# A gated mix of two attentions on one core: tiles of the second half of the values prepared before the weights are loaded, zero rows sent later and from more partitions, two SBUF pools in another order

## The chip, the cores and the metric

The kernel runs on one core of a Trainium2 chip. The metric is the device time of one execution in microseconds. The kernel before took 1667.22 us, the median of three executions (1666.85 to 1672.58). The profile is of one execution with a span of 1664.9 us.

## The reference

Two attention layers read the same input `x` (2048 tokens of 576 values, bf16) and are mixed by a gate.

```python
g = sigmoid((x * gate_w).sum(-1))
a = _A_ref(x, A_mem0, A_Wq, A_Wk, A_Wv, A_Wo, A_seg_len)
b = _B_ref(x, B_wqkv, B_wo)
return g * a + (1 - g) * b
```

- Layer A goes through the tokens in 64 segments of 32, one after the other. To each segment the 8 memory rows that the segment before produced are prepended. Those 40 rows are projected to queries, keys and values (32 heads of 128), attended under a causal mask that always admits the memory rows, and projected back by `Wo`. The first 8 output rows are the next segment's memory. So the segments form a chain.
- Layer B is ordinary full attention over all 2048 tokens with 32 heads of 18 values each. Queries, keys and values are `x @ wqkv`, without a mask, and the output is multiplied by `wo`.

## The kernel before, in words

**Two layers, interleaved.** The order of the instructions on each engine is the order in which the program writes them. Layer A's chain leaves PE idle, so layer B's attention is cut into 512 steps (`b_steps`, a generator) and the steps are placed between layer A's. A step is a block of scores (4 matmuls `sb`, L238), an exponential on ACT (`etb`, L257) and, one step later, 4 matmuls with the values (`ob`, L222). `b_advance` takes one step; `between(cost)` takes one whenever enough cost has been added up.

**The prologue** is everything before the loop over segments, up to about 225 us. This is where the change lies. In order:

1. Loads of `x` by rows of 128 tokens (`xn`, five buffers in pool `pw`) and of B's weights `wb` (L370, L371).
2. Zeros: `zt`, a `stg` tile (three buffers in pool `pw`), is cleared in 4 partitions (L377). Queries and keys of B are kept in DRAM (`qtd`, `ktd`) in groups of four heads, each head in 32 rows of which 18 are used. The other 14 rows of each head of group 0 are zeroed from `zt` by two transfers from POOL's queue, each of 4 heads by 14 rows of 4 KB (L383). POOL then issues five small transfers of `gw` and clears four tiles `vt` (pool `pp`, L392, L393); an entry of 1 in each head's 19th place makes the values' matmul give the softmax sums.
3. A loop over t = 0 to 3, 512 tokens each. `transpose_x` transposes `x` into `xT` and POOL stores it to `xtd` and copies the last 8 tokens of each segment to `xL`. `project_qk` computes blocks 0, 4 and 5 (`FIRST`) of queries and keys with 5 matmuls into a bank `pq` (L422) and casts them to a `stg` tile. `project_vb(0, kb)` computes the first half of the values, 16 heads, with 5 matmuls into `pvb` (L449), casts them into one of the tiles `vts`, and SP stores the tile to `vgd` (L457). Three PSUM banks are used in turn by all of these. Casts go to DVE or ACT by a counter (`copy_out`, L289 and L291).
4. `load_first` puts on SP the loads of the first keys, values and queries of B.
5. Layer A's weights `wv`, `wq`, `wk`: 18 pieces, 14.2 MB, issued by POOL (L106, L108). `in_turn` lets each piece wait until the piece two before it has landed; the first ones wait for the last load of point 4.
6. The gate: 80 small matmuls (L490).
7. `store_qk` of `FIRST` for groups 1 to 7: 15 stores from `stg` on SP.
8. Five more tiles for the values, in the buffers of `xn`, are cleared by POOL (L518, L519). With the four `vt` there are nine. Then `project_vb(1, kb)` for 16 kb computes the second half of the values, starting with the five new tiles.
9. Blocks 1, 6, 2, 7, 3, 8 of queries and keys, 4 times 5 matmuls each, with a step of B between some of them. After each block SP stores it to all groups.
10. The prologue's pools `pw` and `pp` are given back. `wo` (pool `aw2`), `fix` and `seg2` take memory that overlaps theirs, so a first write into them waits for the last reader of the tile that was there.
11. `last_tokens(0)`: layer A's queries, keys and values of the last 8 tokens of 16 segments (L313, L326), cast into `tm` tiles of pool `seg2`.

Every engine and every queue takes its instructions in order, so an instruction that waits holds back all behind it on the same engine. POOL's order in points 5 and 8 is: 18 weight pieces with their waits, then the memsets.

Of the kernel before, what the change touches and what calls it, by code (L numbers as in the profile page):

```python
# [9 lines left out]
BF16 = mybir.dt.bfloat16  # L10
# [6 lines left out]
def kernel(  # L17
# [15 lines left out]
    nc = tc.nc  # L33
    P = nc.NUM_PARTITIONS

    B_, S, Dm = A_x.shape
# [7 lines left out]
    DhB = Dm // HB  # L44
# [37 lines left out]
    qtd = dpool.tile([GB, P, S], BF16, name="qtd")  # L82
    ktd = dpool.tile([GB, P, S], BF16, name="ktd")
# [44 lines left out]
    def bank(k, shape, dtype, name):  # L128

        if k is None:  # L130
            k = turns[0] % 3
            turns[0] += 1
        return ps_a.tile(shape, dtype, name=name, tag=f"b{k}")
# [132 lines left out]
    def load_first():  # L266
        next(bgen)
# [17 lines left out]
    def copy_out(out, in_, share):  # L285

        evac[0] += 1
        if share and evac[0] % share == 0:
            nc.scalar.copy(out=out, in_=in_)  # L289
        else:  # L290
            nc.vector.tensor_copy(out=out, in_=in_)  # L291
# [3 lines left out]
    def load_xlb(q):  # L295
        if q < n_seg // SG:
            xlbs[q] = fil.tile([P, NF + 2, P], BF16, name="xlb", bufs=1)
            nc.sync.dma_start(out=xlbs[q][:, :, :].rearrange("p c t -> p (c t)"), in_=xld[q])
# [53 lines left out]
        ready.append(dma)  # L352

    pctx = ExitStack()
    pp = pctx.enter_context(tc.tile_pool(name="pp", bufs=1, side="right"))
    pw = pctx.enter_context(tc.tile_pool(name="pw", bufs=2, side="right"))
    xT = pp.tile([P, NF + 2, S], BF16, name="xT")
    wb = pp.tile([P, NF + 1, 3 * Dm], BF16, name="wb")
    xL = pp.tile([P, NF + 2, n_seg * LO], BF16, name="xL")
# [3 lines left out]
    def load_x(n, eng):  # L363
        xns[n] = pw.tile([P, Dm], BF16, name="xn", bufs=5)
        eng.dma_start(out=xns[n][:], in_=x_td[n * P:(n + 1) * P, :])
# [8 lines left out]
    nc.vector.memset(xT[0:TL, NF + 1, :], 0.0)  # L374

    zt = pw.tile([P, S], BF16, name="stg", bufs=3)
    nc.vector.memset(zt[0:4, :], 0.0)  # L377

    def pads(t, g):
        return t[g].rearrange("(j r) s -> j r s", r=32)[:, DhB:32, :]  # L380

    for t in (qtd, ktd):
        nc.gpsimd.dma_start(out=pads(t, 0), in_=zt[0:4, :].unsqueeze(1).to_broadcast([4, 32 - DhB, S]))  # L383
    nc.vector.memset(gw[:], 0.0)
    for c in range(NF + 1):
        n = min(P, Dm - c * P)
# [1 line left out]
    HV = HB // 2  # L388
    vts = []
    for i in range(4):  # L390
        vt = pp.tile([P, HV, 32], BF16, name=f"vt{i}")[:, :, :]
# [5 lines left out]
    def transpose_x(n):  # L397
        xn = xns.pop(n)
        ptx = bank(None, [P, NF + 2, P], BF16, "ptx")
        for c in range(NF):  # L400
            nc.tensor.transpose(out=ptx[:, c, :], in_=xn[:, c * P:(c + 1) * P], identity=ident[:, :])
        nc.tensor.transpose(out=ptx[0:TL, NF, :], in_=xn[:, NF * P:Dm], identity=ident[:, :])
        nc.tensor.transpose(out=ptx[:, NF + 1, :], in_=xn[:, T0:Dm], identity=ident[:, :])
        t = slice(n * P, (n + 1) * P)
        nc.vector.tensor_copy(out=xT[:, 0:NF, t], in_=ptx[:, 0:NF, :])
        nc.scalar.copy(out=xT[0:TL, NF, t], in_=ptx[0:TL, NF, :])
        nc.scalar.copy(out=xT[TL:P, NF + 1, t], in_=ptx[TL:P, NF + 1, :])
        nc.gpsimd.dma_start(out=xtd[n].rearrange("p (c t) -> p c t", t=P), in_=xT[:, :, t])
        nc.gpsimd.tensor_copy(
            out=xL[:, :, n * sn * LO:(n + 1) * sn * LO].rearrange("p c (s t) -> p c s t", t=LO),  # L410
            in_=xT[:, :, t].rearrange("p c (s t) -> p c s t", t=seg)[:, :, :, seg - LO:seg],
        )
# [4 lines left out]
    def project_qk(blk, t, share):  # L417
        if t == 0:
            stgs[blk] = pw.tile([P, S], BF16, name="stg", bufs=3)
        pq = bank(None, [P, QC], FP32, "pq")  # L420
        for c in range(NF + 1):
            nc.tensor.matmul(  # L422
                pq[:, :],
                lhsT=wb[:, c, blk * P:(blk + 1) * P],
                rhs=xT[:, c, t * QC:(t + 1) * QC],
                start=(c == 0),
                stop=(c == NF),
            )
        copy_out(stgs[blk][:, t * QC:(t + 1) * QC], pq[:, :], share)

    def store_qk(blk, groups):
        f = blk * P
        while f < (blk + 1) * P:
            which, h, e = f // Dm, f % Dm // DhB, f % DhB
            n = min(DhB - e, (blk + 1) * P - f)
            r = 32 * (h % 4) + e
            if h // 4 in groups:
                nc.sync.dma_start(
                    out=(qtd, ktd)[which][h // 4, r:r + n, :], in_=stgs[blk][f - blk * P:f - blk * P + n, :]
                )  # L440
            f += n


    def project_vb(hf, kb, share):
        vt = vts[(kb + 4 * hf) % len(vts)]
        pv = bank(None, [P, QC], FP32, "pvb")
        c0 = 2 * Dm + hf * HV * DhB
        for c in range(NF + 1):
            nc.tensor.matmul(  # L449
                pv[:, 0:HV * DhB],  # L450
                lhsT=xT[:, c, kb * P:(kb + 1) * P],
                rhs=wb[:, c, c0:c0 + HV * DhB],
                start=(c == 0),
                stop=(c == NF),
            )
        copy_out(vt[:, :, 0:DhB], pv[:, 0:HV * DhB].rearrange("p (h e) -> p h e", e=DhB), share)
        nc.sync.dma_start(  # L457
            out=vgd[kb, :, hf * HV * 32:(hf + 1) * HV * 32], in_=vt.rearrange("p h e -> p (h e)")
        )
# [4 lines left out]
    for t in range(NQC):  # L464
        for n in range(4 * t, 4 * t + 4):
            if n + 4 < NT:
                load_x(n + 4, nc.sync)
            transpose_x(n)
        nc.gpsimd.dma_start(
            out=xld[t].rearrange("p (c t) -> p c t", t=P), in_=xL[:, :, t * P:(t + 1) * P]  # L470
        )
        if t == 0:
            load_xlb(0)
        for blk in FIRST:
            project_qk(blk, t, 2)
        if t == NQC - 1:
            for blk in FIRST:
                store_qk(blk, (0,))
        for kb in range(4 * t, 4 * t + 4):
            project_vb(0, kb, 2)  # L480

    load_first()
    ready.extend([first_loads[-1]] * 2)
# [28 lines left out]

    for blk in FIRST:
        store_qk(blk, range(1, GB))

    for i in range(5):
        vt = pw.tile([P, Dm], BF16, name="xn", bufs=5)[:, 0:HV * 32].rearrange("p (h e) -> p h e", e=32)
        nc.gpsimd.memset(vt, 0.0)  # L518
        nc.gpsimd.memset(vt[:, :, DhB:DhB + 1], 1.0)  # L519
        vts.append(vt)  # L520
    for kb in range(NKB):
        project_vb(1, kb, 3)
    for blk in (1, 6, 2, 7, 3, 8):
# [9 lines left out]
    for q in range(4):  # L533
        in_turn(
            nc.gpsimd.dma_start(
                out=wo[:, 8 * q:8 * q + 8, :], in_=A_Wo[8 * q:8 * q + 8].rearrange("h e d -> e h d")
# [34 lines left out]
    for jj in range(2):  # L571
# [3 lines left out]
            out=cap[o:o + 64, M:L],  # L575
            in_=cap[o:o + 64, M:L],
# [7 lines left out]
            out=cap[o:o + 64, 0:M],  # L584
            in_=cap[o:o + 64, 0:M],
# [460 lines left out]
    for s in range(n_seg):  # L1046
# [6 lines left out]
        for jj in range(2):  # L1053
            nc.sync.dma_start(
                out=v_sb[64 * jj + CT:64 * jj + L, :],
                in_=vld[s * LO:(s + 1) * LO, jj * (HD // 2):(jj + 1) * (HD // 2)],
# [75 lines left out]
```

The softmax here doesn't subtract the row's maximum and nothing guards it: scores larger than these inputs give would overflow.

## Time and profile before

| | |
|---|---|
| median of three executions | 1667.22 us |
| span of the profile | 1664.9 us |
| PE busy | 1476.0 us, 89% |
| ACT busy | 1140.1 us, 68% |
| DVE busy | 960.2 us, 58% |
| POOL busy | 335.8 us, 20% |
| 225 to 1600 us: PE busy, DMA share | 1295.76 of 1375 us, 0.20 |
| 60 to 120 us: PE busy, DMA share | 1.12 of 60 us, 0.80 |

How to read the profile: the page cuts the span into 40 slices of 41.6 us and gives the busy share of each engine in tenths. A table of stretches gives for chosen windows the busy time of each engine with the number of instructions, then the granted clock of PE, the mean share of the 16 DMA engines in use and GB/s. A line of waits reads: who waited (engine, tile, line), for whom, the total in us, how often, the longest. A line in order of time gives start, duration, engine, line, operation, out<-in, and in brackets the idle time before it and what ended it.

### The profile page before, as it was taken

How to read it: one execution, taken by the hardware profiler on the slowest of the kernel's cores; microseconds unless marked ns; L12 is line 12 of the kernel's file. 1: busy time of each engine (PE TensorE's matmuls, PEld its weight loads, DVE VectorE, ACT ScalarE, POOL GpSimd, SP SyncE). 2: the span in 40 equal slices, each digit the busy share in tenths (PEclk: the TensorE clock that was granted, in tenths of full speed). 3: DMA queues.
4: the chain of work that ended last, by engine and by line, in shares of the span. 5: the costliest groups of instructions: out<-in, count | busy, mean ns of one | idle time of the engine just before them, and what ended most of it. 6: DMA issues, size and time to landing. Idle time of an engine off the chain costs nothing.

```text
span 1664.9 us, 57761 instructions
## 1 busy us (share of the span) xinstructions
PE 1476.0 (89%) x25082; PEld 781.3 (47%) x25082; DVE 960.2 (58%) x2355; ACT 1140.1 (68%) x981; POOL 335.8 (20%) x725
## 2 busy tenths in 40 slices
PE   5409789999999999999999999999999989998987
PEld 3204354455555444555545444555554444444445
DVE  2104356666656666666656666666666666565656
ACT  2105567677767777777767777777777788778784
POOL 4320121121313121121213121212121212111031
PEclk9759899999999999999999999999999999999999
DMA  6773532211212212221112122211212121211125
GB/s 177 245 261 99 198 95 63 66 47 44 51 45 49 52 36 59 44 52 39 43 38 65 35 47 51 46 46 35 59 40 51 32 46 30 49 30 33 28 58 162
DMA packets 210089, 114.39 MB, mean 69 GB/s; under 512 B 159715, under 2 KB 197475, under 8 KB 208243
## 3 DMA queue, kind: packets, MB, share of 16 engines
q1 hardware_dynamic: 188971, 58.40, 15.8%
q0 software_dynamic: 19920, 50.02, 9.4%
q8 instruction: 196, 3.21, 0.8%
q10 hardware_dynamic: 944, 2.29, 0.4%
q14 instruction: 58, 0.48, 0.1%
HBM read 60.94 MB, written 36.10 MB: 58 GB/s over the span
## 4 chain that ended last, share of the span: by engine, by line
PE 69%; ACT 11%; DVE 11%; DMA 5%; issue 2%; POOL 1%; SPq 1%; ACTq 0%; DVEq 0%; POOLq 0%
PE pvv L755 26%; ACT etb L257 8%; PE sb L238 8%; PE ob L222 7%; PE pt L782 5%; PE pv L326 4%; PE psh L800 3%; PE acc L643 3%; PE pso L838 2%; PE pq L422 2%; PE pv L313 2%; DVE hl L657 2%; DVE ot L850 2%; DVE hl L654 2%; ACT rq L830 2%
## 5 line engine op out<-in xcount | busy, mean ns | idle before, releaser
L257 ACT ACTIVATE etb<-sb 128x2048 bf16<-128x2048 f32 x512 | 959.6, 1874 | 343.7 <-PE sb L238 343.7
L767 DVE CAST tm<-pvv 128x512 bf16<-128x512 f32 x384 | 264.4, 689 | 173.7 <-PE pvv L755 172.6
L755 PEld LDWEIGHTS <-ht 128*32 128x32 bf16 x7680 | 185.6, 96 | 183.6 <-DVE ht L891 14.1
L238 PE MATMUL sb<-qch,kch 32*128 32x512 bf16 x2048 | 203.7, 386 | 37.7 <-ACT etb L257 35.7
L222 PE MATMUL ob<-etb,vch 128*32 128x512 bf16 x2048 | 206.2, 392 | 0.8 <-DVE tq L159 0.8
L850 DVE CAST ot<-pso 128x320 bf16<-128x320 f32 x256 | 120.7, 488 | 104.8 <-PE pso L838 100.5
L643 PE MATMUL acc<-wo,ot 128*32 128x384 bf16 (+1 forms) x4096 | 160.3, 291 | 5.5 <-DVE ot L850 3.3
L755 PE MATMUL pvv<-wq_m,ht 128*32 128x512 bf16 x2048 | 134.6, 383 | 13.0 <-DVE ht L891 8.5
L755 PE MATMUL pvv<-wv_m,ht 128*32 128x512 bf16 x2048 | 134.5, 383 | 0.0
L755 PE MATMUL pvv<-wk_m,ht 128*32 128x512 bf16 x2048 | 133.5, 381 | 0.0
L643 PEld LDWEIGHTS <-ot 128*32 128x32 bf16 x4096 | 105.4, 98 | 46.7 <-DVE ot L850 12.9
L700 POOL DMA_DIRECT2D a_dram<-rl x186 | 92.6, 506 | 163.9 <-DVE rl L695 143.3
L238 PEld LDWEIGHTS <-kch 32*128 32x128 bf16 x2048 | 61.1, 91 | 126.7 <-issue 106.5
L857 POOL COPY otl<-ot 128x256 bf16<-128x256 bf16 x64 | 25.9, 405 | 445.1 <-DVE ot L850 445.1
L222 PEld LDWEIGHTS <-vch 128*32 128x32 bf16 x2048 | 52.9, 93 | 118.0 <-issue 116.2
L782 PE MATMUL pt<-ident,tm 128*128 128x128 bf16 x1024 | 96.8, 221 | 0.8 <-DVE tm L767 0.8
L838 PE MATMUL pso<-et,v_sb 64*128 64x40 bf16 x2048 | 81.4, 178 | 14.3 <-DVE hll L657 5.3
L790 DVE COPY kt<-pt 128x512 bf16<-128x512 bf16 x128 | 54.0, 422 | 69.4 <-PE pt L782 69.1
L838 PEld LDWEIGHTS <-v_sb 64*128 64x128 bf16 x2048 | 62.9, 93 | 62.0 <-issue 49.8
L654 DVE CAST hl<-acc 128x384 bf16<-128x384 f32 (+1 forms) x128 | 57.9, 452 | 57.7 <-PE acc L643 57.5
L782 PEld LDWEIGHTS <-tm 128*128 128x128 bf16 x1024 | 57.8, 98 | 67.0 <-issue 49.4
L826 ACT ACTIVATE lt<-pss 128x320 f32<-128x320 f32 x128 | 56.0, 438 | 43.4 <-PE pss L822 32.8
(141 smaller groups left out, 1841.2 us busy)
## 6 DMA issues: line engine op xcount, KB each, us to landing
v_sb<-tm SPq DMA_DIRECT2D x512, 32.0 KB
wo<-in_A_Wo_dram POOLq DMA_DIRECT2D x4, 1152.0 KB, 8.6
wv_m<-in_A_Wv_dram POOLq DMA_DIRECT2D x4, 1024.0 KB, 7.6
wq_m<-in_A_Wq_dram POOLq DMA_DIRECT2D x4, 1024.0 KB, 5.4
wk_m<-in_A_Wk_dram POOLq DMA_DIRECT2D x4, 1024.0 KB, 5.8
xl<-qld SPq DMA_DIRECT2D x64, 64.0 KB
xl<-kld SPq DMA_DIRECT2D x64, 64.0 KB
v_sb<-vld SPq DMA_DIRECT2D x128, 32.0 KB
```

What stands on the lines that cost most here:

```text
L222: nc.tensor.matmul(ob[32 * j:32 * j + 32, :], lhsT=vc[:, o + 32 * j:o + 32 * j + 32], rhs=et4[:, j, :], start=(kb == 0), stop=(kb == NKB - 1),
L238: nc.tensor.matmul(sb[:, j, :], lhsT=kc[32 * j:32 * j + 32, o:o + P], rhs=qch[gq][32 * j:32 * j + 32, :], start=True, stop=True, tile_posi ...
L257: nc.scalar.activation(out=before[:, :, :], in_=sb[:, :, :], func=ACT.Exp, scale=scale_b)
L326: nc.tensor.matmul(pv[:, o:o + P], lhsT=lw, rhs=xlb[:, cc, :], start=(c == 0), stop=(c == NF))
L643: nc.tensor.matmul(acc[32 * j:32 * j + 32, 0:d1 - d0], lhsT=o[:, h, 0:CT], rhs=wo[:, h, d0:d1], start=(b == 0 and i == 0), stop=(b == 1 an ...
L654: nc.vector.tensor_copy(out=hl[:, 0, d0:d1], in_=acc[:, 0:d1 - d0])
L700: eng.dma_start(out=rows4[m, seg - LO:seg, i * n:(i + 1) * n], in_=rl[32 * i + m * LO:32 * i + (m + 1) * LO, :],)
L755: nc.tensor.matmul(pv[32 * j:32 * j + 32, :], lhsT=ht[:, cc, :], rhs=rw, start=(c == 0), stop=(c == NF), tile_position=(0, 32 * j),)
L767: nc.vector.tensor_copy(out=sbt[x][:, :], in_=ps[x][:, :])
L782: nc.tensor.transpose(out=pt[:, which, :, :, :].rearrange("p j (u i) t -> p j u i t", i=4)[:, :, :, i, :], in_=sbt[x][:, i * Dh:(i + 1) * Dh],
L838: nc.tensor.matmul(pso[:, i * L:(i + 1) * L], lhsT=v_sb[64 * jj:64 * jj + 64, b * 1024 + i * Dh:b * 1024 + (i + 1) * Dh], rhs=et[64 * jj:6 ...
L850: nc.vector.tensor_copy(out=ot[:, j * HG:(j + 1) * HG, :].rearrange("p h t -> p (h t)"), in_=ps["o", b, jj][:, 0:W8],)
```

## The change

Four edits, all in the prologue; what is computed stays the same.

- The five further tiles for the values are cleared before `load_first` and before the weights' pieces in the program's order, so on POOL the memsets stand ahead of the pieces. They are meant to be ready when the second half of the values is projected.
- The zero rows of group 0 are sent after the first four tiles of `x` have been stored (inside the loop, at t = 0), in eight transfers of 14 rows.
- Each of these reads 14 partitions of the zero tile instead of 4 partitions that are read 14 times; the tile is cleared in 14 partitions.
- Pool `pw` is opened before pool `pp`, which exchanges their places in SBUF, and with that which later tiles lie on whose old bytes.

```diff
     pctx = ExitStack()
+    pw = pctx.enter_context(tc.tile_pool(name="pw", bufs=2, side="right"))
     pp = pctx.enter_context(tc.tile_pool(name="pp", bufs=1, side="right"))
-    pw = pctx.enter_context(tc.tile_pool(name="pw", bufs=2, side="right"))
...
     zt = pw.tile([P, S], BF16, name="stg", bufs=3)
-    nc.vector.memset(zt[0:4, :], 0.0)
+    nc.vector.memset(zt[0:32 - DhB, :], 0.0)
...
-    for t in (qtd, ktd):
-        nc.gpsimd.dma_start(out=pads(t, 0), in_=zt[0:4, :].unsqueeze(1).to_broadcast([4, 32 - DhB, S]))
...
         if t == 0:
             load_xlb(0)
+            for r in range(8):
+                nc.gpsimd.dma_start(out=pads((qtd, ktd)[r // 4], 0)[r % 4], in_=zt[0:32 - DhB, :])
...
+    for i in range(5):
+        vt = pw.tile([P, Dm], BF16, name="xn", bufs=5)[:, 0:HV * 32].rearrange("p (h e) -> p h e", e=32)
+        nc.gpsimd.memset(vt, 0.0)
+        nc.gpsimd.memset(vt[:, :, DhB:DhB + 1], 1.0)
+        vts.append(vt)
 
     load_first()
     ready.extend([first_loads[-1]] * 2)
...
     for blk in FIRST:
         store_qk(blk, range(1, GB))
-
-    for i in range(5):
-        vt = pw.tile([P, Dm], BF16, name="xn", bufs=5)[:, 0:HV * 32].rearrange("p (h e) -> p h e", e=32)
-        nc.gpsimd.memset(vt, 0.0)
-        nc.gpsimd.memset(vt[:, :, DhB:DhB + 1], 1.0)
-        vts.append(vt)
     for kb in range(NKB):
         project_vb(1, kb, 3)
```

## The prediction

> **What bounds the kernel now.** I read the page's slices first, then the busy table of single stretches, the waits, the chain of waits and the queues.
>
> ```profile
> PE   5409789999999999999999999999999989998987
> ...
> 60.00:120.00 60.00, 1.12 (x10) 0.76 (x8) 0.17 (x1) 0.00 (x0) 9.81 (x19) 0.54 0.80 276
> 120.00:132.00 12.00, 11.14 (x67) 7.81 (x67) 4.65 (x11) 2.00 (x5) 2.90 (x10) 0.72 0.50 166
> 132.00:172.00 40.00, 37.43 (x233) 14.01 (x231) 16.99 (x25) 26.28 (x14) 0.36 (x1) 1.00 0.26 79
> 172.00:182.50 10.50, 3.72 (x27) 1.40 (x27) 0.00 (x0) 3.75 (x2) 2.36 (x3) 0.79 0.81 270
> ```
>
> From slice 5 on PE is nine tenths busy: the 64 segments are bound by PE, and the change doesn't touch them. The holes are in the prologue. The columns of the stretches are PE, PEld, DVE, ACT and POOL busy, then PE clock, DMA share, GB/s. From 60 to 120 us every engine but POOL stands still while 276 GB/s come in (the A weights); at 172 there is a second hole. A time saved before 225 us is saved at the end, as the segments run the same work from wherever they start.
>
> The waits name the causes (engine and line, waited for: total, times, longest):
>
> ```profile
> DVE xn L291 <- POOL xn L518: 61.2, 3, 60.2
> PE pvb L449 <- DVE xn L291: 59.7, 1, 59.7
> PE pq L422 <- DMA wb<-in_B_wqkv_dram: 14.6, 4, 9.5
> POOL xtd L408 <- DMA qtd<-stg: 11.5, 1, 11.5
> DVE tm L291 <- DMA ktd<-stg: 10.7, 1, 10.7
> ```
>
> The first two are the big hole: the second half's projections wait for a memset, not for weights. POOL's order of time shows why:
>
> ```profile
> 119.26 0.52 POOL L108 DMA_DIRECT2D wk_t<-in_A_Wk_dram  x1 [2.66 <-DMA wk_m<-in_A_Wk_dram]
> 119.77 0.54 POOL L518 MEMSET xn<- 128x512 bf16 x1
> 120.37 0.17 POOL L519 MEMSET xn<- 128x16 bf16 x1
> ```
>
> The memset stands behind the 18 weight issues, each of which waits for the piece two before it. PE then runs from 120.86. The third wait is the loading of wb; the last is the hole at 172: `tm` (pool seg2) lies on bytes of the old `stg` tiles, so its cast waits for their last store.
>
> From 18 to 20 us (queue: packets, MB, share of 16 engines) only the zero rows on q0 keep the queues busy:
>
> ```profile
> q0 software_dynamic: 12, 0.05, 41.7%
> q1 hardware_dynamic: 13, 0.01, 2.1%
> q10 hardware_dynamic: 5, 0.01, 1.7%
> ```
>
> That is 0.417 x 16 x 2 / 12 = 1.1 us a packet on 6.7 engines; q10 carries the end of wb. From 3 to 7 us q10 took 0.676 x 64 / 404 = 0.11 us a packet.
>
> [...] So SP's small stores will share with 8 KB weight rows; the trace has that at 72 to 76 us. [...]
>
> **The change part by part**, in times of the kernel before.
>
> (a) Zero rows. Gone: two transfers before wb. By 12 us 3.1 MB had moved, nearly all of x and wb, so wb should be in at about 13 us, not 24. New: eight 14-row transfers behind the first four xtd stores, and the cast of block 5 at t = 0 needs the zero tile's buffer (three `stg` buffers: zero, 0, 4, then 5 on the zero's). DVE waits there, and behind it stand the casts that free PE's banks. POOL: gw issues end at 7.3 instead of 8.8 (0.80 + 0.64 less), four memset pairs 2.7 us to 10.0, four store and copy pairs at 1.0 to 14.5, xld to 15.5, eight issues at 0.55 to 0.8 to 19.9 or 21.9, landing 2.6 (as xtd) to 3.5 us (as an 18-row store): 22.5 to 25.4. The cast ended at 29.35; now 23.2 to 26.1. Gain 3.3 to 6.2, taken 5. Ends: 0 if the rows move at the old 40 GB/s, 8 if the Pool part is quicker. The larger memset costs nothing: 0.91 us for 4 partitions, as for 64 (L373).
>
> (b) Memsets ahead of the weights. 5 x 0.7 = 3.5 us of POOL after the last xld (56.5), done by 60. The weights don't start later: POOL stood 12.1 us before L106, waiting for the first key and value loads. PE can run the second half from 59. Its nine tiles (five xn, four vt) take kb 0 to 8; kb 9 needs kb 0's store landed, and that store stands on SP behind 15 stores of FIRST, issued until 71.5. In the trace those go on landing until about 80 under the weights' first pieces (q1 48 packets at 74 to 76, 52 at 76 to 78). So kb 9 at 80, and one tile for each store landed up to kb 15. [...] Unhindered 0.56 us (issue pace at L457)[...]. Estimate 1.5: part of the time q0 has gaps. 80.5 + 6 x 1.5 = 89.5. The half ended at 131.9: gain 42. Ends: 79 (stores land 2.5 us after issue) and 97.5 (2.9 each), so 53 and 34.
>
> (c) Blocks 1, 6, 2, 7, 3, 8: 40 us as before (PE 37.4 of 40), now under weight traffic. Block 7 needs block 1's stores landed 13 us after it ended; under `wo` a block's stores took 10.6 us (171.8 to 182.4). Loss 2, ends 0 and 6.
>
> (d) Pool order. `tm` now lies where pp's tiles were, read long ago; instead `wo` waits for `stg`'s last store, which only moves a load needed 60 us later. 10.7 us go, less the three banks that PE filled meanwhile (3 x 1.1 us, part paid): gain 8, ends 6 and 10.7.
>
> (e) Warmer PE at 182 (clock 0.79 for 10 us): 1.5. The rest is order and names: nothing.
>
> Sum: 5 + 42 - 2 + 8 + 1.5 = 54.5; 1667.2 - 54.5 = 1612.7, say 1613. All low ends: 0 + 34 - 6 + 6 + 0 = 34, 1633. All high: 8 + 53 + 10.7 + 1.5 = 73, 1594.
>
> Do the weights then become the bound? They landed at about 122. SP's 4.2 MB beside them (16 x 128 KB and four blocks' stores), at 375 GB/s, add at most 11: 133. The path reaches `last_tokens` at 90 + 42 = 132; wv and wq are in by then, wk is used some 22 us later. Slack 20 us, so no.
>
> **The rivals.**
> 1. SP's stores starve behind the weights until these end (128 to 133): block 7 waits for block 1's stores until 130, three blocks of 6.6 follow, 150 instead of 171.8. 22 + 5 + 8 = 35: 1632. For: q1 fell to 16 packets in 72 to 74. Against: few were left to send; q0 has gaps. Chance 0.18.
> 2. The weights are slowed by over 25 us and `last_tokens` waits for wk: 1640. For: DMA share is 0.80 already. Against: the slack above. 0.05.
> 3. Slower. The zero rows' new wait on DVE, with 40 GB/s, delays t = 0 by some 5 us, and the freed window stays closed by another wait on POOL or SP: 1672. For: DVE and SP serve in order, and six more POOL issues stand ahead. Against: no queue entry ahead of the memsets depends on the weights. 0.03.
> 4. No change because what fills the window is taken back by the segments: they would have to be bound by a transfer, but have a DMA share of 0.20 and PE at 94%. 0.02.
>
> **How the numbers follow.** Forecast 0.72 at 1613; the range reaches to rival 1 and near to the high ends: 1597 to 1632. Faster by over 0.5%: 0.72 + 0.18 + 0.05 = 0.95; same 0.02; slower 0.03.
>
> **What would show it.** PE idle at 60 to 120 broken up: projections of the second half up to kb 8 by about 60, a wait of DVE or ACT for a vgd store (not POOL) of 10 to 20 us, pq blocks from about 85. DVE's wait for `qtd<-stg` in t = 0, wb in at 13 us. No wait of `tm` for `ktd<-stg`. The weights' last issue a few us later than 119. I am wrong if blocks 7, 3, 8 show long waits for stores (rival 1), if L313 or L326 wait for a weight load (rival 2), or if the segments' part is no longer 1375 us for the same work.

## The result, and the profile after

The changed kernel takes 1618.32 us (median, 1615.62 to 1619.57), beside 1669.9 us of the kernel before on the same chip: ratio 0.9687, 95% interval 0.9658 to 0.9716. That is 51.6 us less, between 47 and 57 by the interval. Forecast were 1613 us and 54.5 less, with a range of 1597 to 1632. The profiled span fell from 1664.9 to 1613.9 us.

First the page's PE slices of the changed kernel, then its table of stretches (PE, PEld, DVE, ACT and POOL busy, PE clock, DMA share, GB/s):

```profile
PE   6598899999999999999999999999999989998997
```

```profile
57.00:66.00 9.00, 5.88 (x48) 4.56 (x47) 2.36 (x6) 1.03 (x3) 0.00 (x0) 1.00 0.75 213
66.00:80.00 14.00, 1.16 (x6) 0.70 (x6) 0.92 (x2) 0.40 (x1) 2.17 (x4) 0.50 0.91 298
80.00:100.00 20.00, 18.42 (x110) 7.90 (x108) 8.10 (x13) 9.79 (x6) 2.69 (x5) 0.92 0.92 317
100.00:120.00 20.00, 18.95 (x122) 7.08 (x119) 8.30 (x12) 13.60 (x8) 2.68 (x5) 1.00 0.79 262
120.00:140.00 20.00, 15.08 (x88) 5.55 (x87) 7.45 (x13) 10.81 (x6) 3.96 (x6) 0.95 0.85 298
```

The 60 us in which only POOL worked have shrunk to a hole of 16 us in PE's work, from 63 to 79 us. From 80 on PE computes while the weights come in. From the seventh slice on, the PE slices are what they were but for one digit.

The waits of the changed kernel up to 190 us that the argument needs:

```profile
ACT xn L289 <- DMA vgd<-xn: 17.8, 1, 17.8
DVE xn L291 <- DMA vgd<-xn: 16.9, 2, 16.7
PE pvb L447 <- DVE xn L291: 16.0, 1, 16.0
DVE stg L291 <- DMA ktd<-stg: 8.0, 1, 8.0
DVE tm L291 <- DMA qld<-tm: 7.2, 4, 2.5
DVE tm L291 <- DMA vld<-tm: 4.3, 1, 4.3
PE pq L420 <- DMA wb<-in_B_wqkv_dram: 3.9, 4, 2.0
```

The wait for POOL's memset is gone, and so is `tm`'s for `ktd<-stg`; `ktd<-stg` appears instead at the cast of block 5, which waits for the zero rows (the forecast had named `qtd<-stg`; the rows of `ktd` go last). In place of the memset the tenth value tile (kb 9) waits for a store, 17 us instead of 60. And `tm` waits for the stores of `last_tokens` itself. In the order of time the new hole looks like this, on DVE and then on POOL:

```profile
61.15 0.46 DVE L291 CAST vt<-pvb 128x288 bf16<-128x288 f32 x1 [0.84 <-PE pvb L447]
78.33 0.46 DVE L291 CAST xn<-pvb 128x288 bf16<-128x288 f32 x1 [16.71 <-DMA vgd<-xn]
```

```profile
55.56 0.53 POOL L484 MEMSET xn<- 128x512 bf16 x1
56.14 0.17 POOL L485 MEMSET xn<- 128x16 bf16 x1
66.37 1.11 POOL L106 DMA_DIRECT2D wv_m<-in_A_Wv_dram  x2 [10.05 <-DMA vch<-vgd]
```

The memsets end at 56; POOL still stands 10 us before the first weights, so they cost nothing.

To see where the time came from I read when the same five instructions start in the two traces:

| point (us) | before | after | earlier by |
|---|---|---|---|
| first transpose of the loop's second round | 30.91 | 26.41 | 4.5 |
| last cast of the values' second half | 131.93 | 86.13 | 45.8 |
| last cast of blocks 1 to 8 | 171.10 | 123.42 | 47.7 |
| end of `last_tokens` (memset of `cap`, L568) | 221.95 | 170.28 | 51.7 |
| first cast of segment 0 (L767) | 228.69 | 176.17 | 52.5 |
| end | 1664.9 | 1613.9 | 51.0 |

From the first cast of segment 0 to the end it is 1436.2 us before and 1437.7 after. In all the kernels below it is 1436 to 1442, so differences are read at the points of the prologue, and a difference of 2 or 3 us between medians says little. The points themselves come from one trace each, and they scatter too: the kernel with `wo` held back (below) is the same program up to the end of the blocks, and its trace has the last cast of the values' second half at 88.3 us and the last cast of the blocks at 127.25, that is 2.2 and 3.8 us later than the changed kernel's. A difference of up to 4 us at one point doesn't count by itself.

### The profile page after: what moved, and what is told of

Same layout as the page of the kernel before. It is cut to its first block, busy times and chain, and to the rows that moved or that the text cites. A ratio compares the mean times of both kernels' runs of the same rounds, so it can differ in the third digit from the quotient of the medians.

```text
span 1613.9 us, 57766 instructions
## 1 busy us (share of the span) xinstructions
PE 1476.7 (91%) x25082; PEld 782.0 (48%) x25082; DVE 960.0 (59%) x2355; ACT 1139.8 (71%) x981; POOL 338.4 (21%) x731
## 3 DMA queue, kind: packets, MB, share of 16 engines
q10 hardware_dynamic: 944, 2.29, 0.4%
## 4 chain that ended last, share of the span: by engine, by line
PE 69%; ACT 11%; DVE 11%; DMA 4%; issue 2%; SPq 1%; POOL 1%; DVEq 0%; ACTq 0%; POOLq 0%
PE pvv L755 27%; ACT etb L257 9%; PE sb L238 8%; PE ob L222 7%; PE pt L782 5%; PE pv L326 4%; PE psh L800 3%; PE acc L643 3%; PE pso L838 3%; PE pv L313 2%; DVE hl L657 2%; PE pq L420 2%; DVE hl L654 2%; DVE ot L850 2%; ACT rq L830 2%
## 5 line engine op out<-in xcount | busy, mean ns | idle before, releaser
L767 DVE CAST tm<-pvv 128x512 bf16<-128x512 f32 x384 | 264.4, 689 | 175.1 <-PE pvv L755 174.2
```

Of the source, the lines that this page charges most:

```text
L767: nc.vector.tensor_copy(out=sbt[x][:, :], in_=ps[x][:, :])
```

## The experiments

**One part at a time.** Each of the first three is the kernel before with one of the edits that the diff shows; the fourth is the changed kernel without one.

Memsets alone:

```diff
+    for i in range(5):
+        ...
+        nc.gpsimd.memset(vt, 0.0)
+        nc.gpsimd.memset(vt[:, :, DhB:DhB + 1], 1.0)
+        vts.append(vt)
     load_first()
...
     for blk in FIRST:
         store_qk(blk, range(1, GB))
-    for i in range(5):
-        ...
-        nc.gpsimd.memset(vt, 0.0)
-        nc.gpsimd.memset(vt[:, :, DhB:DhB + 1], 1.0)
-        vts.append(vt)
```

> The kernel before with only the memsets of the five tiles moved ahead of the weights. Theory (the gains add up by stage): the second half of the values gains 40 us and the blocks after it 2, the zero rows and the wait of tm for ktd<-stg stay, so 40 to 44 us less than before, about 1626. Rival (the pool order is needed to harvest it): under the weights the stores of stg land so late that tm's wait grows from 10.7 to over 20 us, and the gain is 30 us or less, about 1638.

1628.58 us, ratio 0.9751 (0.973 to 0.9772): 41 us less. As in the theory; the rival's long wait didn't come:

```profile
DVE xn L291 <- DMA vgd<-xn: 19.7, 3, 16.7
DVE tm L291 <- DMA ktd<-stg: 9.4, 1, 9.4
```

So this edit is four fifths of the gain, the wait for the store belongs to it, and `tm`'s old wait stays at 9.4 us. From the last cast of the blocks to the end of `last_tokens` it takes 50.9 us, as in the kernel before.

Zero rows alone:

```diff
-    nc.vector.memset(zt[0:4, :], 0.0)
+    nc.vector.memset(zt[0:32 - DhB, :], 0.0)
...
-    for t in (qtd, ktd):
-        nc.gpsimd.dma_start(out=pads(t, 0), in_=zt[0:4, :].unsqueeze(1).to_broadcast([4, 32 - DhB, S]))
...
             load_xlb(0)
+            for r in range(8):
+                nc.gpsimd.dma_start(out=pads((qtd, ktd)[r // 4], 0)[r % 4], in_=zt[0:32 - DhB, :])
```

> The kernel before with only the zero rows' edit. Theory: wb lands by 13 us, the loop starts its second round about 4 us earlier, and so does all that follows, the weights too: 3 to 4 us less than before. Rival (the wait for the weights hides it): no change, 0 to 1 us.

1665.18 us, ratio 0.9978 (0.9968 to 0.9989): 4 us less. The second round starts at 27.07 us (30.91 before) and segment 0's first cast at 225.97 (228.69). So the wait for the weights doesn't hide the gain.

Pools alone:

```diff
-    pp = pctx.enter_context(tc.tile_pool(name="pp", bufs=1, side="right"))
     pw = pctx.enter_context(tc.tile_pool(name="pw", bufs=2, side="right"))
+    pp = pctx.enter_context(tc.tile_pool(name="pp", bufs=1, side="right"))
```

> The kernel before with only the two pools exchanged. Theory as predicted: tm's wait of 10.7 us for ktd<-stg goes and 8 to 9.5 us are gained. Rival (from the changed kernel, where this stage gained only about 4): last_tokens now runs while wo is loaded, its stores vld, qld and kld land late, and tm waits for them instead; 3 to 5 us are gained.

1665.28 us, ratio 0.997 (0.9954 to 0.9987), between 2 and 8 us less. The median can't tell theory from rival. The trace, which is of the fastest of eight executions, shows more: from the last cast of the blocks to the end of `last_tokens` it takes 43.5 us (171.55 to 215.05) instead of 50.9 (171.10 to 221.95). The wait of 10.7 is gone and 7.4 are kept, a little less than the theory's 8 to 9.5, as `tm` now waits for its own stores:

```profile
DVE tm L291 <- DMA qld<-tm: 6.9, 2, 4.3
DVE tm L291 <- DMA vld<-tm: 2.8, 2, 2.3
```

The changed kernel with the old pools:

> The changed kernel with the pools in the old order. Theory: tm waits again for the last store of stg, 5 to 10 us, part of which is won back because the stores of last_tokens then meet less weight traffic: 4 to 8 us slower than the changed kernel. Rival (the pool order does nothing once the memsets have moved): the same within 1 us.

1621.51 us, ratio 0.9708 (0.968 to 0.9736); its interval overlaps the changed kernel's. So the times alone don't decide. In the trace `tm` waits for `ktd<-stg` again, and the stretch from the blocks to the end of `last_tokens` takes 52.6 us instead of 46.9, 5.7 us more:

```profile
DVE tm L291 <- DMA ktd<-stg: 10.8, 1, 10.8
```

This speaks against the rival: the four traces with the old pools have 50.9 to 52.6 us in this stretch, the changed kernel and the three below that differ from it only in the loop 44.2 to 48.3. The three single gains add up to 49 us (41 + 4 + 4); together the edits gave 51.6.

**What the new wait of 17 us is made of.** SP's order alone:

```diff
-    for blk in FIRST:
-        store_qk(blk, range(1, GB))
     for kb in range(NKB):
         project_vb(1, kb, 3)
+    for blk in FIRST:
+        store_qk(blk, range(1, GB))
```

> The changed kernel with the 15 stores of FIRST placed behind the second half of the values on SP instead of ahead of it. Theory (the new wait of 17 us for vgd<-xn is mostly a matter of SP's order: that store stands behind 15 others): the wait falls to 6 us or less, the half is done 8 to 14 us earlier, block 1 then waits some us for the stores of FIRST, and the kernel is 3 to 8 us faster than the changed one. Rival (the weights' traffic alone makes the stores land late): the wait stays over 12 us and the time within 2 us.

1618.23 us, ratio 0.9696 (0.9663 to 0.973): no difference from the changed kernel. The first half of the theory holds, the wait falls from 16.9 to 4.6 us. But block 1 then waits 10.7 for the stores that were put back:

```profile
DVE stg L291 <- DMA ktd<-stg: 10.7, 1, 10.7
DVE xn L291 <- DMA vgd<-xn: 4.6, 2, 4.3
```

The blocks end at 122.15 instead of 123.42. A wait was turned into another, as the same 15 stores have to land either way.

The weights held back:

```diff
-    for d in pieces:
-        in_turn(d)
...
     for kb in range(NKB):
         project_vb(1, kb, 3)
+    ready.extend([vstores[-1]] * 2)
+    for d in pieces:
+        in_turn(d)
```

(`vstores[-1]` is the last store of the values, on which the pieces are made to wait.)

> The changed kernel with the weights' pieces held until the last store of the values' second half has landed. Theory (order on SP and weight traffic share the wait): without weight traffic the wait for vgd<-xn is about 10 us instead of 17, the half ends near 77 us; the weights start at about 82 instead of 66 us and end near 148, so last_tokens waits for wk and the whole is 0 to 8 us slower than the changed kernel. Rival (the weights have ample slack): no wait for wk, and it is faster by 5 us or more. If the weights play no part in the wait, it stays at 17 us.

1617.02 us, ratio 0.9683 (0.9667 to 0.97), the same. The wait is 10.8 us:

```profile
DVE xn L291 <- DMA vgd<-xn: 10.8, 2, 10.6
```

So of the 17 us some 11 remain without the weights, by SP's order, and 6 go with the weights' traffic. The blocks end 7 us earlier, at 116.33, and the end of `last_tokens` is the same to 0.7 us (169.63): the stretch takes 53.3 us instead of 46.9. Neither theory nor rival had that. The weights' first issue came 13.6 us later (79.95) and no wait of PE for a weight shows. The waits of `tm` for its own stores are what grew, from 11.5 to 19.5 us:

```profile
DVE tm L291 <- DMA vld<-tm: 7.3, 2, 6.5
DVE tm L291 <- DMA kld<-tm: 6.4, 2, 3.8
DVE tm L291 <- DMA qld<-tm: 5.8, 3, 2.0
```

**What holds `last_tokens`.** `wo` held back:

```diff
-    for q in range(4):
-        in_turn(
-            nc.gpsimd.dma_start(out=wo[:, 8 * q:8 * q + 8, :], ...)
-        )
...
     for i, _ in enumerate(last_tokens(0, 1 << 30)):
         if i % 2:
             between(1.1)
+    ready.extend([lstores[-1]] * 2)
+    for q in range(4):
+        in_turn(
+            nc.gpsimd.dma_start(out=wo[:, 8 * q:8 * q + 8, :], ...)
+        )
```

(`lstores[-1]` is the last store of `last_tokens`.)

> The changed kernel with the loading of wo held until the last store of last_tokens has landed. Theory (what the pool order gained is partly given back because vld, qld and kld land late beside wk and wo): the casts into tm wait less for qld, last_tokens takes 40 us or less instead of 46, and wo comes at about 190 us, just in time or a few us late: 0 to 6 us faster than the changed kernel. Rival (the waits come from wk or from SP's issue pace): last_tokens stays at 45 us and nothing is gained, or wo comes late and it is slower by up to 10 us.

1634.74 us, ratio 0.98 (0.9776 to 0.9824), 16 us slower than the changed kernel. The waits for `qld` are gone, and 6.0 us for `vld` are left of 11.5 in all, but the stretch takes 44.7 us (127.25 to 171.91), only 2.2 less. PE is busy for 39.9 us of it in the changed kernel and has the same matmuls here, so little could be gained behind those waits. What made it slow is what stands behind `wo` on POOL (the trace puts `wo`'s wait down to the load of `xlb`, which SP issued right behind the last store):

```profile
174.52 1.86 POOL L551 DMA_DIRECT2D wo<-in_A_Wo_dram  x2 [39.63 <-DMA xlb<-xld]
182.45 0.88 POOL L551 DMA_DIRECT2D wo<-in_A_Wo_dram  x1 [6.07 <-DMA wo<-in_A_Wo_dram]
185.51 0.88 POOL L551 DMA_DIRECT2D wo<-in_A_Wo_dram  x1 [2.18 <-DMA wo<-in_A_Wo_dram]
186.40 0.22 POOL L576 TENSOR_SCALAR_AFFINE_SELECT cap<-cap 64x32 bf16<-64x32 bf16 x1
186.56 0.20 POOL L585 TENSOR_SCALAR_AFFINE_SELECT cap<-cap 64x8 bf16<-64x8 bf16 x1
```

The masks, the clearing of `v_sb` and segment 0's tokens follow behind; segment 0's first cast comes at 192.39 instead of 176.17. My edit had built the fault that the change under study removes. The expectation saw only when `wo` would land.

SP's order and `wo` held back, both together:

> The edits of the two kernels with the stores of FIRST behind the values and with wo behind last_tokens, together, on the changed kernel. Theory: both gains add, 3 to 14 us faster than the changed kernel, less where the earlier last_tokens runs into the end of wk. Rival: last_tokens waits for wk by as much as it starts earlier, and only the gain of wo's edit is left.

1631.49 us, ratio 0.9772 (0.9755 to 0.9788). The blocks end at 121.17, `last_tokens` at 172.41: 51.2 us, with waits of 9.1 us for `vld`. It started earlier, beside more of the weights, and took longer; why is left open below. POOL's order then costs the same as above.

More weights:

```diff
-        for c in range(NF):
+        for c in (0, 1, 2, 3, 0):
             yield nc.gpsimd.dma_start(out=w[0][:, c, :], in_=w2[c * P:(c + 1) * P, :])
```

> The changed kernel with one piece of 1 MB of each of wv, wq and wk loaded a second time (3.1 MB more, same values). Theory (after the change the prologue from 66 to 170 us is bound by its transfers, which is why earlier values or later weights moved its end by no more than 2 us): 3.1 MB at the 0.3 MB/us of that stretch push the end of last_tokens back by 8 to 11 us, and the kernel is that much slower than the changed one. Rival (the weights have some 20 us of slack, as the prediction had it, and PE or the order of SP's stores is the bound): 0 to 3 us slower.

1623.77 us, ratio 0.9719 (0.9703 to 0.9735), 5.5 us above the changed kernel. `last_tokens` ends at 176.49 instead of 170.28, 6.2 us later. The weights were through 10.8 us later (the `wo` issue that waits for the last piece comes at 148.77 instead of 137.93). Of the 6.2 us 2.1 stand already at the end of the blocks (125.52) and 4.1 are in `last_tokens`, where the waits of its casts for their own stores grew from 11.5 to 18.9 us:

```profile
DVE tm L291 <- DMA qld<-tm: 12.3, 5, 5.5
DVE tm L291 <- DMA vld<-tm: 6.6, 1, 6.6
```

The theory's 8 to 11 was too much and the rival's 0 to 3 too little: this speaks for a cost of the weights' traffic, through the stores beside it, of about 2 us a MB and not the full 3.3. It isn't firm: the two intervals just overlap, and 4 us is what single traces scatter by.

**The zero rows: form or place.** New form at the old place:

```diff
+    for r in range(8):
+        nc.gpsimd.dma_start(out=pads((qtd, ktd)[r // 4], 0)[r % 4], in_=zt[0:32 - DhB, :])
     nc.vector.memset(gw[:], 0.0)
...
-            for r in range(8):
-                nc.gpsimd.dma_start(out=pads((qtd, ktd)[r // 4], 0)[r % 4], in_=zt[0:32 - DhB, :])
```

> The changed kernel with the zero rows sent at their old place, ahead of everything on POOL, but in the new form of eight transfers from 14 partitions. Theory (both the form and the place count[...]): the rows are through by 14 us, wb lands at 14 to 16 us, block 5 doesn't wait for them, and the second round of the loop starts at 22 to 25 us instead of 26.4, 2 to 4 us earlier. Rival (the place is what counts): wb lands at over 20 us as in the kernel before, and the round starts at about 30 us.

1619.73 us, ratio 0.9709 (0.9674 to 0.9745), the same. The form alone unblocks wb: the last of its chunks is in at 14.0 us, and the second round starts at 20.35, 6 us earlier than in the changed kernel. But the first tile of the second half is filled at 56.10, against 56.61. SP gives a part of the 6 us back, standing at the load of `xlb` until `xld` has landed, with the loads of `x` for the third round behind it:

```profile
SPq L298 <- DMA xld<-xL: 16.4, 1, 16.4
24.07 0.33 SPq L298 DMA_DIRECT2D xlb<-xld  x1
24.51 3.94 SPq L457 DMA_DIRECT2D vgd<-vt  x4
28.54 2.66 SPq L365 DMA_DIRECT2D xn<-in_A_x_dram  x4
```

At the start of the third round 3.8 of the 6.1 us are left (32.09 instead of 35.89). Most of the rest goes in that round with slower matmuls: 13 of `pq` from 36.76 on take 5.08 us, where in the changed kernel 15 from 38.93 on take 3.41. From its first matmul of `pq` to its first of `pvb` the round takes 5.7 us instead of 3.3.

Old form at the new place:

```diff
-            for r in range(8):
-                nc.gpsimd.dma_start(out=pads((qtd, ktd)[r // 4], 0)[r % 4], in_=zt[0:32 - DhB, :])
+            for tt in (qtd, ktd):
+                nc.gpsimd.dma_start(out=pads(tt, 0), in_=zt[0:4, :].unsqueeze(1).to_broadcast([4, 32 - DhB, S]))
```

> The changed kernel with the zero rows at their new place but in the old form, two transfers of 4 partitions read 14 times. Theory (a packet from the four partitions takes 1.1 us whatever else runs): wb lands by 13 us, but block 5's cast waits for the zero rows until about 32 us, so the second round starts at about 34 us, 7 us later than in the changed kernel. Rival (the old form was slow only because it ran beside wb and x): the rows land by 24 us and the second round starts within 1 us of the changed kernel.

1631.59 us, ratio 0.9781 (0.9752 to 0.9809), 13 us slower. Block 5 waits 20 us, and the second round starts at 38.59. From 28 to 30 us nothing else is moved:

```profile
DMA packets 12, 0.05 MB, mean 25 GB/s; under 512 B 0, under 2 KB 0, under 8 KB 12
q0 software_dynamic: 12, 0.05, 43.6%
```

0.436 x 32 / 12 = 1.16 us a packet, with the engines otherwise free. So the packets aren't slow through other traffic. The new place needs the new form, while the new form at the old place does as well as the changed kernel: of the two edits to the zero rows the form is what counts.

The step that suggested itself: rows early in the new form, and `xlb` out of the way.

```diff
         if t == 0:
-            load_xlb(0)
...
     load_first()
+    load_xlb(0)
```

> The changed kernel with the zero rows at their old place in the new form, and with SP's first load of xlb moved from the loop's first round to behind the first key and value loads. Theory (with the zero rows early the second round started 6 us earlier, and SP, standing at xlb's load for xld, took that back in the third round): the loop ends about 5 us earlier, load_first and the weights start that much earlier, and the kernel is 4 to 6 us faster than the changed one. Rival (POOL's later xtd stores or the traffic take it back elsewhere): the same within 2 us.

1614.59 us, ratio 0.9665 (0.9645 to 0.9685). The second round starts at 20.66, the first tile of the second half is filled at 53.30 (56.61 in the changed kernel), `last_tokens` ends at 165.94 (170.28) and segment 0's first cast comes at 172.81 (176.17). So the trace is 3.4 us ahead at that point, which is within the scatter of single traces; the profiled span is 1613.5 and the interval overlaps the changed kernel's: not shown to be faster.

## Why the prediction was right

**(a) Zero rows: 5 forecast, 4.5 measured** at the second round, 3.8 at the fourth (matmuls of `pq` from 47.66 instead of 51.42). The steps hold one by one, within 1.5 us: wb is in at 14.5 us where 13 was said (the 3.1 MB that had moved by 12 us were nearly all of wb and of the half of `x` that had been asked for, not of all `x`), the rows land at 23.6 (22.5 to 25.4), the cast of block 5 ends at 24.5 (23.2 to 26.1). Why the packets of the old form are slow was not shown. At the new place with nothing else moving they came to 25 GB/s in all, with 7.0 engines counted as busy (43.6% of 16 at 28 to 30 us), while in the kernel before a packet of the weights, mostly 8 KB, took 0.31 us at 72 to 74 us (q0: 94 packets, 90.7% of 16 engines), 26 GB/s for one engine. So the 7 engines together moved no more than one moved there, and too few engines alone don't account for it. The new form changes the number of partitions and the repeated reading of the same four rows at once, and may change the number of engines; no run changed one of them alone.

**(b) Memsets: 42 forecast, 42.0 measured** (45.8 less 3.8). In times of the kernel before, kb 9 was put at 80.5 and came at 82 (78.3 + 3.8), the last cast of the half at 89.5 and came at 89.9 (86.13 + 3.8). That it fits to the tenth is luck: the second trace of the same program, 2.2 us later at this point, gives 39.8. The mechanism holds, with 40 to 42 us. Of the wait that took the place of POOL's, the forecast said 10 to 20 us for a `vgd` store behind 15 others; it is 17, and the runs split it into 11 and 6. The 1.5 us for each later tile was an estimate, with an upper end of 2.9 that rested on an assumption that no trace shows; the six tiles after kb 9 took 1.3 us each (78.33 to 86.13).

**(c) Blocks: a loss of 2 forecast, a gain of 1.9 measured** (47.7 less 45.8). The blocks waited 1.4 us for a store in all, so the loss didn't come. The gain fits an overlap: PE had done the first groups and the first scores while the last value casts were waiting, and DVE then cast three in a row at 86.51. But it is within the scatter: the blocks take 37.3 us here, 38.9 in the second trace of the same program and 39.2 in the kernel before.

**(d) and (e) Pools and warm clock: 9.5 forecast, 4.0 measured** (51.7 less 47.7), and 0.8 more before segment 0. This is the mis-sized term. Alone, the pools gave 7.4 in that stretch, the warm clock included (five matmuls `pv` at 182.41 us took 1.20 us; in the kernel before five at 183.25 took 2.29, at a granted clock of 0.50 from 182 to 186 us); in the changed kernel 4.0 (granted clock 0.96 from 123.42 to 170.28 us), or 5.7 against the changed kernel with the old pools. The forecast's sentence "Slack 20 us, so no" looked only at when the weights land. In that it was right: `wk` was first used at 155.69, some 18 us after the last piece had landed (137.93 at the latest), and no wait of PE for a weight shows. But one of its signs failed: the weights' last issue was to come a few us after 119 and came at 134.34, and they ended 20 us later than before (in times of the kernel before), where at most 11 were said from a rate of 375 GB/s; the stretches from 80 us on have 262 to 317. So most of `wk` came in beside `last_tokens` as well as `wo`, and the forecast left out what such traffic may do to its small stores, on which the four `tm` buffers wait (11.5 us in the changed kernel). I had reckoned with it for the `vgd` stores and not for `vld` and `qld`. The waits of `tm` growing from 11.5 to 18.9 us with 3.1 MB more agree with it, within the limits said there. A rival isn't excluded: the first `vld` stores (128.73) also stand on SP behind eight stores of the last block (124.14 to 127.87), and no run took these away.

Sum: 3.8 + 42.0 + 1.9 + 4.0 + 0.8 = 52.5 up to segment 0, and 1.5 lost after it, within the scatter there. The total is as close as it is partly by luck: the blocks came out 3.9 better than forecast and the pools and the clock 4.7 worse, and the two nearly cancel.

**The rivals.** Stores starved until the weights end: no, the wait of the blocks for stores is 1.4 us. Weights as the bound of `last_tokens`: not by landing late; that their traffic costs some us is likely, not firmly shown. Slower through DVE's new wait: the wait is 8 us and covered by wb's earlier arrival; with the old form it is 20. No change: the segments took nothing back (1436.2 and 1437.7 us).

**Left open:** why the part with `vld` takes longer when it starts earlier (9.1 us of waits in the combined kernel against 4.3). Weight traffic and the order on SP both fit, and no run separates them there.

## What to carry to other kernels

A cheap instruction that needs nothing from a long chain of throttled transfers shouldn't stand behind it on the same queue: look for an engine that waits for a memset or a copy while only transfers run, and read what stands ahead of it (here DVE waited 60.2 us for a memset of 0.54 us behind 18 pieces). Once the hole is open, look at the next queue: here the order on SP made up some 11 of the 17 us that were left. And look at transfers that run beside the freed work twice: for when they land, and for what they may do to the small stores that free its buffers (here those waits went from 11.5 to 18.9 us with 3.1 MB more).

## What the runs showed that was not expected

- The old form of the zero rows at the new place, which reads four partitions over and over, moved 25 GB/s in all (1.16 us for 4 KB) even with nothing else under way, with some 7 engines counted as busy. The two transfers took 18.6 and 18.7 us to land. From 14 partitions the same 0.46 MB were through 7.6 us after the first issue (16.0 to 23.6), with other transfers beside them.
- Four changes of order in the freed stretch (stores after values, weights later, `wo` later, the two combined) ended `last_tokens` at 168.5, 169.6, 171.9 and 172.4 us, against 170.3, though the blocks before it ended between 116 and 127. So 7 us won at the end of the blocks (116.33) weren't kept in `last_tokens`.
- Sending the zero rows early in the new form won 6 us in the second round, of which 0.5 were left at the end of the loop: SP's wait of 16.4 us took one part, slower matmuls in the third round (13 in 5.08 us instead of 15 in 3.41) another.
